# Warm products in the head, two more port users in the planner, and new rank shifts in a planned attention kernel

## The chip, the cores and the metric

The kernel runs on one core of a Trainium2 chip. The metric is the device time of one execution in microseconds (us); of several runs the median is given. A core has five engines that run beside each other: TensorE (PE, matrix products), VectorE (DVE), ScalarE (ACT), GpSimd (POOL) and SyncE (SP, which here only issues transfers).

## The reference

Both branches read the same x (2048 tokens of 512 numbers), and a gate per token mixes them. There are 32 heads of width 16.

```python
g = sigmoid((x * gate_w).sum(-1, keepdims=True))
# branch A: softmax attention
q, k, v = split_heads(x @ A_wqkv)
a = merge(softmax(q @ k.T * 16 ** -0.5) @ v) @ A_wo
# branch B: linear attention with a learned feature map
q, k, v = split_heads(x @ B_wqkv)
phi = lambda t: concat(softmax(t @ w_phi), softmax(-(t @ w_phi)))
kv, z = phi(k).T @ v, phi(k).sum(tokens)
b = merge(phi(q) @ kv / (phi(q) @ z + 1e-6)) @ B_wo
out = g * a + (1 - g) * b
```

The bulk is in branch A: 32 heads x 2048 x 2048 scores, each to be exponentiated.

## The kernel before, in words

**Units.** The scores are cut into units: 128 keys by 512 queries of one head. Four units (four heads, one in each strip of 32 rows of TensorE) for one tile of keys are a "pack"; 16 packs make a group, and there are 32 groups (4 blocks of queries by 8 sets of four heads). A unit takes a score product (`_scores`, L1015), an exponential, and a value product (`_values`, L1122).

**Two ways to the exponential.** Most units go through ScalarE, two at a time: `_qk` makes a score group of two units in the banks 0 to 3 of the accumulation memory, `_exp` (L1063) exponentiates both in one instruction. Score group k waits for exponential k-2, whose bank it takes over. The other units, 488 of 2048, go through VectorE: one instruction (L922) turns a score tile into the bits of a 16-bit float, and steps on four tiles at a time (L947) refine them; the value products then read the tiles `vs`. `NUMS` says how many units of each group take this way. The first score groups are made by halves of the 512 queries, since x lands in halves.

**The head.** `_warm` (L689) issues nine products that nobody reads while the first half of x is on its way. `_proj_k0` (L706) and `_proj_q0` (L745) project keys and queries of the first 512 tokens in two halves of four products each. ScalarE and VectorE (L757, L753) bring the queries into `qT`, VectorE casts the keys into `kT` (L735; later tiles of keys by L770).

**Padding.** Where the planner believes that TensorE has done too little in the last 3 us, it puts up to two products that nobody reads into a score group (`o.pad`, L1035), from score group `PADK` on; they are issued after the group's wait. Within the value products it adds quartets with zero weights (`_fill`, L1129).

**The gate.** `_gate` projects x onto `gate_w`: `gw` is spread to `gwb` by a VectorE copy (L832), four products and transposes follow, an exponential, and at last four small VectorE copies (L862, named `gate_b`) into `ghB`, which branch B reads in its second half.

**The planner.** The order of all instructions is not written by hand. Every step becomes an operation with an engine, an estimated duration, a rank (`prio`, mostly the number of the pack by which it is due) and what it depends on. `order` (a list scheduler) plays all five engines with these estimates, and takes the operation that could start first; among those ready at the same time, the one of the lowest rank. VectorE and GpSimd share a port to the on-chip memory: an operation of GpSimd, or one of VectorE whose name is in `PORT`, starts in the plan only when the last such one has ended. `shift` adds a pseudo-random amount of up to 1, 2 or 3 to the ranks, drawn by one seed in `SEEDS` for each 16 packs of rank (0: no shift). What comes out is a fixed queue for each engine; the waits between them are semaphores, worked out from the dependences. So any change of a rank, a duration or a rule redeals the order from that point on.

Of the kernel before, what the change touches and what calls it, by code (L numbers as in the profile page):

```python
# [10 lines left out]
P = 128  # L11
# [54 lines left out]
class Plan:  # L66
# [43 lines left out]
    def op(self, eng, fn, cost, reads=(), writes=(), deps=(), name="", prio=0.0, rel=-99, kind="full",  # L110
           acquire=None, release=None, lat=None, array=None, strips=None, also=None):
        o = Op(eng, fn, cost, name, prio, rel, kind, self.LAT[eng] if lat is None else lat)
        found = {}
        for b in reads:
            for w in b.writers:
                found[id(w)] = w
        for b in writes:
            for w in b.readers or b.writers:
                found[id(w)] = w
            if b.readers:  # L120
                for w in b.writers:
                    found[id(w)] = w
        for d in deps:
            if d is not None:
                found[id(d)] = d
        found.pop(id(o), None)
        o.deps = list(found.values())
        for b in reads:
            b.readers.append(o)
        for b in writes:  # L130
            b.writers, b.readers = [o], []
        o.acquire, o.release, o.also = acquire, release, also
        o.strips = strips
        o.port = eng == "POOL" or eng == "DVE" and name in self.PORT
        o.held = eng == "PE" and acquire is None and name in self.HOLDING
        o.array = cost if array is None else array
        self.ops.append(o)
        return o

    SEEDS = (6713, 8236, 795, 8928, 4203, 3987, 4548, 4431, 3369, 6855, 1992, 9096, 3816, 673, 8476, 4153, 2488, 5053, 9892, 380, 9864, 6961, 8928, 7398, 8610, 6258, 6732, 8778, 7190, 2318, 6568, 0, 527, 0)  # L140

    def shift(self):
        count = {}
        for o in self.ops:
            k = count[o.name] = count.get(o.name, 0) + 1
            s = self.SEEDS[min(max(int(o.prio // 16), 0), 33)] if o.prio >= 0 else 0
            if s:
# [26 lines left out]
    SAME = 100  # L174
    OPEN = 2
    HURRY, FREE = 20, 30
    PORT = ("v_step", "b_neg", "b_max", "b_sub", "b_sum", "b_total", "b_mul", "n_mul", "n_den", "kvbd")
    HOLDING = ("kproj", "qproj", "bv", "pq", "vproj", "outa", "outb", "wtr", "xtr")

    def rank(self, o):  # L180
# [227 lines left out]
class _Kernel:  # L408
# [18 lines left out]
    VMIN = 8  # L427
    FAST = 3
    VSOON = -2
    PADK = 8  # L430
    LAST, FIRST_OUT, NEXT_OUT, DEP_OUT = 0, 8, 0, 2
    ALONE, EARLY = 12, 10
    PVP = 10
# [248 lines left out]
        job.bank = bank  # L682
        return job, (job if bank is None else None)

    def _warm(self, n, after):

        def run(e):
            for _ in range(n):
                ins = e.matmul(self.ps[:, 4, :], self.warm[:, 0:P], self.warm[:], start=True, stop=True)  # L689
            return ins  # L690
        self.plan.op("PE", run, 0.427 * n, reads=[self.b_warm], deps=[after], name="warm", prio=-99)

    COLS = 0

# [44 lines left out]
    def _proj_q0(self, half, bank):  # L739

        lo, op, ends = 256 * half, self.plan.op, []
        job, pool = self._job(bank)
        m = None
        for c in range(4):
            m = op("PE", lambda e, c=c: e.matmul(self._bank(job)[:, 0:256], self.WA[:, 0, c, 0:P],  # L745
                                                 self.xT[:, c, lo:lo + 256], start=(c == 0), stop=(c == 3)),
                   self.c_pe(256), reads=[self.b_x0[half], self.b_WA[0][0]], deps=[m], name="qproj", prio=half - 2.2,
                   acquire=None if c else pool)
            m.urgent = half - 99
        for side in range(2):  # L750
            dst, by = self.qT[:, side, lo:lo + 256], self.mask[:, side:side + 1]
            if half or side:
                o = op("DVE", lambda e, dst=dst, by=by: e.tensor_scalar(dst, self._bank(job)[:, 0:256], by, None,  # L753
                                                                        op0=ALU.mult), self.c_dve(256) + 0.06,
                       deps=[m] + ends, reads=[self.b_mask], name="q0_ev", prio=side - 2, release=pool if side else None)
            else:
                o = op("ACT", lambda e, dst=dst, by=by: e.activation(dst, self._bank(job)[:, 0:256], ACT.Copy, scale=by),  # L757
                       self.c_act(256) + 0.1, deps=[m], reads=[self.b_mask], name="q0_ev", prio=-2)
            self.b_qT[side].writers.append(o)
            if side == 0:  # L760
                self.b_q0[half].writers.append(o)
            ends.append(o)
        self.early.setdefault(bank, []).extend(ends)

    def _proj_k(self, cp, j):
        due = 32 * cp + 3 * j - self.KDUE if cp else 4 * j - 2.0
        self._proj(lambda c: self.WA[:, 1, c, P * cp:P * cp + P],
                   lambda c: self.xT[:, c, QCH * j:QCH * j + QCH],
                   [self.b_xT[j], self.b_WA[1][cp > 0]],
                   [lambda e, b: e.tensor_copy(self.kT[:, cp, QCH * j:QCH * j + QCH], b)],  # L770
                   self.c_dve(512), due, due - (24 if cp else 99), "kproj", [self.b_kT[cp][j]],
                   urgent=32 * cp + 4 * j - self.SOON)
# [92 lines left out]
                prio=100))  # L865
        self.b_gB.writers = done

    NUMS = (6, 10, 12, 14, 14, 15, 13, 16, 13, 20, 17, 13, 16, 13, 19, 21, 10, 18, 12, 16, 19, 13, 17, 16, 15, 20, 12, 19, 17, 16, 23, 13)

    def _plan_vector(self):  # L870

        NT, away = self.NT, []
        for g in range(self.NPACK // NT):
            n = self.NUMS[g]
            rest = self.REND if g == self.NPACK // NT - 1 else self.REST
# [151 lines left out]
    def _qk(self, a, b, half=None):  # L1027
# [22 lines left out]
        o.on_commit = commit  # L1050
        o.pad = k >= self.PADK
        self.qks.append(o)
# [594 lines left out]
```

## Time and profile before

| | |
|---|---|
| median of 3 runs | 767.77 us (766.18 to 769.58) |
| the profiled execution's own time | 767.62 us |
| its span, first to last instruction | 765.6 us |
| mean granted TensorE clock | 0.997 |
| busy: PE, ACT, DVE, POOL | 97%, 98%, 93%, 27% of the span |
| exponentials of scores on ACT | 782 |
| score tiles by DVE (L922) | 488 |

A row of a group of instructions gives line, engine, operation, output and input, count, then busy time and mean length of one, then the idle time of the engine ahead of them and what ended it. A row of the timeline gives start, length, engine, line and count of instructions merged. A row of a window gives its bounds and length, then for each engine the busy time and count, then the granted clock, the share of the transfer engines and the bandwidth. A wait's row gives who waited for whom: total, times, longest. In rows of one line or tile, three numbers with slashes are the shortest, median and longest duration in ns. A product's end is modelled, so products overlap in the rows.

### The profile page before, as it was taken

The page shows a single profiled execution, that of the slowest core. Times are in us where ns is not written, and L with a number is a line of the kernel's source. Part 1 is how long each engine was busy: PE and PEld are TensorE (multiplying, and loading weights), DVE is VectorE, ACT ScalarE, POOL GpSimd, SP SyncE. Part 2 cuts the span into 40 slices and gives each one's busy share as a digit, 9 for nine tenths or more (in the row PEclk, how much of TensorE's full clock was granted, in tenths as well). Part 3 has the DMA queues.
Part 4 walks back from the last instruction along what each step waited for, and adds up shares of the span by engine and source line. Part 5 has one row for each costly group of instructions (what it writes and reads, how often), then busy time and mean ns, then how long its engine had stood idle before and what let it go on. Part 6 is the DMA issues. An engine that isn't in the chain of part 4 may idle for free.

```text
span 765.6 us, 17042 instructions
## 1 busy us (share of the span) xinstructions
PE 739.6 (97%) x7149; PEld 219.6 (29%) x7220; DVE 711.6 (93%) x1110; ACT 749.1 (98%) x804; POOL 207.5 (27%) x301
## 2 busy tenths in 40 slices
PE   8999999999999999999999999999999999999998
PEld 3322233222222222222332322232222222222222
DVE  4778997899999999999999999999999999999995
ACT  6999999999999999999999999999999999999996
POOL 2210255315053260405145023422314140250000
PEclk9999999999999999999999999999999999999999
DMA  9501001000000000010121202211111121011000
GB/s 232 127 2 28 3 14 15 1 2 8 9 3 14 1 3 14 1 15 2 15 29 28 53 11 51 45 27 30 32 26 28 29 47 24 15 30 27 5 12 28
DMA packets 89180, 20.78 MB, mean 27 GB/s; under 512 B 83472, under 2 KB 88592, under 8 KB 89104
## 3 DMA queue, kind: packets, MB, share of 16 engines
q1 hardware_dynamic: 87232, 18.92, 13.4%
q8 instruction: 56, 0.92, 0.5%
q10 hardware_dynamic: 1872, 0.79, 0.4%
q14 instruction: 20, 0.16, 0.1%
HBM read 4.21 MB, written 2.10 MB: 8 GB/s over the span
## 4 chain that ended last, share of the span: by engine, by line
ACT 76%; PE 15%; DVE 9%; issue 1%
ACT ET L1063 73%; PE ps L1015 5%; PE ps L1122 5%; PE ps L698 3%; ACT bq L1310 3%; DVE vs L922 3%; DVE vs L947 2%; PE ps L1129 1%; PE ps L689 1%; DVE onB L1475 1%; DVE T L1143 0%; DVE bq L1307 0%; DVE btree L1304 0%; DVE ghB L862 0%; DVE qtmp L783 0%
## 5 line engine op out<-in xcount | busy, mean ns | idle before, releaser
L1063 ACT ACTIVATE ET<-ps 128x1024 bf16<-128x1024 f32 (+1 forms) x782 | 720.4, 1154 | 3.7 <-PE ps L1015 3.6
L922 DVE TENSOR_SCALAR vs<-ps 128x512 uint16<-128x512 f32 x488 | 313.7, 679 | 20.7 <-PE ps L1015 19.7
L1015 PE MATMUL ps<-qT,kT 32*128 32x512 bf16 (+1 forms) x2052 | 312.4, 385 | 13.1 <-ACT ET L1063 8.0
L947 DVE TENSOR_SCALAR vs<-vs 128x2048 uint16<-128x2048 uint16 (+1 forms) x244 | 235.4, 977 | 1.9 <-PE ps L1122 0.5
L1122 PE MATMUL ps<-vs,V 128*32 128x512 bf16 x1952 | 216.4, 384 | 1.4 <-DVE vs L947 1.4
L1122 PE MATMUL ps<-ET,V 128*32 128x512 bf16 x1560 | 194.5, 387 | 0.1
L1015 PEld LDWEIGHTS ps<-qT,kT 32*128 32x128 bf16 x2052 | 78.0, 91 | 309.3 <-ACT ET L1063 293.2
L1314 POOL TENSOR_TENSOR btree<-btree 128x512 f16<-128x512 f16 (+1 forms) x32 | 33.4, 1044 | 188.8 <-DVE btree L1312 188.0
L1122 PEld LDWEIGHTS ps<-ET,V 128*32 128x32 bf16 x1560 | 48.9, 94 | 84.1 <-issue 75.8
L1129 PE MATMUL ps<-kT,zero 128*32 128x512 bf16 x628 | 63.4, 385 | 0.0
L1122 PEld LDWEIGHTS ps<-vs,V 128*32 128x32 bf16 x1952 | 49.8, 95 | 45.9 <-issue 27.5
L1299 POOL TENSOR_SCALAR bq<-bq 128x1024 bf16<-128x1024 bf16 x16 | 21.5, 1341 | 150.6 <-DVE bq L1281 119.5
L698 PE MATMUL ps<-WB,xT 128*128 128x512 bf16 x160 | 49.6, 383 | 2.8 <-issue 2.1
L1160 POOL TENSOR_TENSOR T<-T,rinv 128x512 bf16<-128x512 f32 x15 | 18.2, 1210 | 83.4 <-DVE rinv L1158 83.2
L698 PE MATMUL ps<-xT,WA 128*128 128x512 bf16 x101 | 33.2, 392 | 1.9 <-issue 1.6
L788 POOL TENSOR_SCALAR qT<-qtmp,mask 128x512 bf16<-128x512 bf16 x30 | 25.8, 866 | 28.8 <-DVE qtmp L783 28.5
L1143 DVE STREAM_TRANSPOSE T<-ps 128x512 f32<-128x512 f32 x32 | 22.6, 707 | 11.2 <-PE ps L1122 11.1
L1310 ACT ACTIVATE bq<-bq 128x2048 bf16<-128x2048 bf16 x16 | 32.1, 2007 | 0.2
L1281 DVE CAST bq<-ps 128x512 bf16<-128x512 f32 x32 | 21.7, 680 | 0.3 <-PE ps L698 0.2
L826 POOL TENSOR_SCALAR V<-V 128x544 bf16<-128x544 bf16 x16 | 12.6, 788 | 33.4 <-DVE V L819 33.2
L698 PEld LDWEIGHTS ps<-WB,xT 128*128 128x128 bf16 x192 | 13.3, 97 | 25.3 <-issue 20.5
L1129 PEld LDWEIGHTS ps<-kT,zero 128*32 128x32 bf16 x628 | 14.7, 94 | 19.7 <-issue 18.8
(88 smaller groups left out, 405.3 us busy)
## 6 DMA issues: line engine op xcount, KB each, us to landing
T<-T SPq DMA_DIRECT2D x240, 8.0 KB, 1.8
WB<-in_B_wqkv_dram SPq DMA_DIRECT2D x1, 1536.0 KB, 7.9
out_dram<-WB SPq DMA_DIRECT2D x12, 128.0 KB, 1.7
WA<-in_A_wqkv_dram SPq DMA_DIRECT2D x2, 384.0 KB, 5.4
WoB<-in_B_wo_dram SPq DMA_DIRECT2D x1, 512.0 KB, 3.8
WoA<-in_A_wo_dram SPq DMA_DIRECT2D x1, 512.0 KB, 4.8
WA<-in_A_wqkv_dram ACTq DMA_DIRECT2D x2, 128.0 KB, 3.1
WA<-in_A_wqkv_dram ACTq DMA_DIRECT2D x1, 256.0 KB, 4.6
```

What stands on the lines that cost most here:

```text
L698: return e.matmul(out, lhs, rhs, start=start, stop=stop)
L788: x = self.plan.op("POOL", lambda e, side=side: e.tensor_scalar(self.qT[:, s0 + side, :], tmp, self.mask[:, side:side + 1], 0.0, op0=ALU.m ...
L922: bits = lambda e, to, src: e.tensor_scalar(to, src, SCALE * LOG2E * 128.0, float(ORIGIN), op0=ALU.mult, op1=ALU.add)
L947: o = op("DVE", lambda e, k=k, src=src, dst=dst: e.tensor_scalar(dst, src, float(STEPS[k - 1]), None, op0=ALU.add), 0.16 + k * n * QCH * 0 ...
L1015: return e.matmul(out[:, cols], self.kT[32 * i:32 * i + 32, cp, kt * TOK:(kt + 1) * TOK], self.qT[32 * i:32 * i + 32, s, cols], start=True ...
L1063: o = plan.op("ACT", lambda e: e.activation(self.ET[:, a % NS:a % NS + n, cols], self.ps[:, a % NR:a % NR + n, cols], ACT.Exp, scale=SCALE ...
L1122: ins = e.matmul(self._bank(ot)[32 * i:32 * i + 32, :], v[:, v0:v0 + 32], tile, start=(kt == 0), stop=(kt == self.NT - 1), tile_position=( ...
L1129: ins = e.matmul(self._bank(ot)[32 * i:32 * i + 32, :], self.zero[:], self.kT[:, 0, 0:QCH], start=False, stop=False, tile_position=(0, 32 ...
L1143: t1 = op("DVE", lambda e: e.transpose(T1[:, side].rearrange("p b s -> p (b s)"), src()), 0.735, deps=last, writes=[b_T1[side]], name="n_t ...
L1281: [lambda e, b, k=k: e.tensor_copy(bq[:, k].rearrange("p (g s v) -> p g s v", g=8, s=2)[:, :, 0, :], b.rearrange("p (g v) -> p g v", g=8))],
L1310: op("ACT", lambda e: e.activation(flat, flat, ACT.Exp), 1.789, reads=[b], writes=[b], name="b_exp", prio=due + 1)
L1314: + [("b_sum", two(128 * n), lambda e, n=n: e.tensor_tensor(half[:, :, 0:n], half[:, :, 0:n], half[:, :, n:2 * n], ALU.add), (n <= self.P_ ...
```

## The change

It does five things:

- `_proj_q0` adds, after the four products of the first half, an operation of three warm products into bank 1 (`WARM = 3`, rank -2.15, estimated at 0.215 us each). The first score group that uses bank 1 depends on it; both are on TensorE, so no semaphore is waited for.
- `gate_b` and `gwb` join the names in `PORT`.
- `PADK` goes from 8 to 2, so padding is allowed from score group 2 on.
- All 34 seeds of the rank shifts are other ones.
- `NUMS` moves one unit from group 16 to group 15 and one from group 31 to group 30 (counted from 0); the total stays 488.

```diff
-    SEEDS = (6713, 8236, 795, 8928, 4203, 3987, 4548, 4431, 3369, 6855, 1992, 9096, 3816, 673, 8476, 4153, 2488, 5053, 9892, 380, 9864, 6961, 8928, 7398, 8610, 6258, 6732, 8778, 7190, 2318, 6568, 0, 527, 0)
+    SEEDS = (4012, 8099, 2555, 4405, 246, 6853, 8703, 3994, 8542, 8480, 8579, 1442, 8131, 8756, 6763, 9811, 0, 3602, 7438, 1689, 2615, 6046, 0, 2892, 1945, 7535, 9937, 2713, 4648, 6479, 9995, 0, 4360, 0)
...
-    PORT = ("v_step", "b_neg", "b_max", "b_sub", "b_sum", "b_total", "b_mul", "n_mul", "n_den", "kvbd")
+    PORT = ("v_step", "b_neg", "b_max", "b_sub", "b_sum", "b_total", "b_mul", "n_mul", "n_den", "kvbd", "gate_b", "gwb")
...
-    PADK = 8
+    PADK = 2
...
-    def _warm(self, n, after):
+    def _warm(self, n, after, bank=4, cost=0.427, prio=-99):
 
         def run(e):
             for _ in range(n):
-                ins = e.matmul(self.ps[:, 4, :], self.warm[:, 0:P], self.warm[:], start=True, stop=True)
+                ins = e.matmul(self.ps[:, bank, :], self.warm[:, 0:P], self.warm[:], start=True, stop=True)
             return ins
-        self.plan.op("PE", run, 0.427 * n, reads=[self.b_warm], deps=[after], name="warm", prio=-99)
+        return self.plan.op("PE", run, cost * n, reads=[self.b_warm], deps=[after], name="warm", prio=prio)
+
+    WARM = 3
...
         self.early.setdefault(bank, []).extend(ends)
+        if self.WARM and not half:
+            self.early.setdefault(1, []).append(self._warm(self.WARM, m, bank=1, cost=0.215, prio=-2.15))
...
-    NUMS = (6, 10, 12, 14, 14, 15, 13, 16, 13, 20, 17, 13, 16, 13, 19, 21, 10, 18, 12, 16, 19, 13, 17, 16, 15, 20, 12, 19, 17, 16, 23, 13)
+    NUMS = (6, 10, 12, 14, 14, 15, 13, 16, 13, 20, 17, 13, 16, 13, 19, 22, 9, 18, 12, 16, 19, 13, 17, 16, 15, 20, 12, 19, 17, 16, 24, 12)
```

In the order that is built, the queue of TensorE grows by 19 products: the three warm ones and four quartets of `_fill`. The pads in score groups stay three in number, two of them now in score group 4 and one late, where before there was one in each of three late groups. The numbers of instructions on the other engines stay, and their order differs almost everywhere.

## The prediction, made before the changed kernel ran

> **What bounds the kernel now.** I read the page first: the shares of the engines, the chain that ended last, the costliest groups.
>
> ```profile
> span 765.6 us, 17042 instructions
> ...
> PE 739.6 (97%) x7149; PEld 219.6 (29%) x7220; DVE 711.6 (93%) x1110; ACT 749.1 (98%) x804; POOL 207.5 (27%) x301
> ...
> ACT 76%; PE 15%; DVE 9%; issue 1%
> ...
> L1063 ACT ACTIVATE ET<-ps 128x1024 bf16<-128x1024 f32 (+1 forms) x782 | 720.4, 1154 | 3.7 <-PE ps L1015 3.6
> ```
>
> ScalarE (ACT) is busy for 98% of the span and owns 76% of the chain; one kind of instruction, the exponential of a pair of score tiles, is 720 of its 749 us. Next I asked what ACT waited for, over the whole run.
>
> ```profile
> ACT xT L1596 <- remote: 3.8, 1, 3.8
> ACT ET L1063 <- PE ps L1015: 3.6, 6, 1.4
> ACT qT L757 <- PE ps L745: 3.5, 1, 3.5
> ACT L657 <- issue: 2.3, 1, 2.3
> ```
>
> So 9.6 us lie at the two ends (table load, first projection, last output) and only 3.6 us in six waits between. But "busy" hides something: exponentials overlap, and one that starts a little late still counts as busy without a break. The timeline gives the true pace, and the grouped lines of 18 to 757 us the load:
>
> ```profile
> 720.02 14.78 ACT L1063 ACTIVATE ET<-ps 128x1024 bf16<-128x1024 f32 x16
> 734.49 2.15 ACT L1063 ACTIVATE ET<-ps 128x1024 bf16<-128x1024 f32 x2
> ...
> L1063 ACT ACTIVATE ET<-ps 128x1024 bf16<-128x1024 f32 x772 | 712.4, 1158 | 2.1 <-PE ps L1015 2.1
> L1310 ACT ACTIVATE bq<-bq 128x2048 bf16<-128x2048 bf16 x16 | 32.1, 2007 | 0.2
> ```
>
> Sixteen exponentials stand between the starts 720.02 and 734.49: 0.904 us each, undisturbed. 772 of them make 697.9 us. The 16 long ones take 2.007 us less the overlap of about 0.25 that the others show (1.158 - 0.904), an estimate of 1.75, together 28.0. That is 726 of the 739 us in this stretch (739.0 = 757 - 18): some 13 us are lost to late starts, of which 2.1 show as waits. This, the head and the tail are all that a change of order can touch. The built order of the changed kernel holds the same 782 exponentials, 16 long ones and 488 VectorE (DVE) tiles, so ACT's own work stays. TensorE (PE) gets 3 warm products and 4 more filler quartets; both are off the path except where I price them.
>
> **Part one, the head: warm products, and padding from the second score group on.**
>
> ```profile
> 1.45 4.02 PE L689 MATMUL ps<-warm 128*128 128x512 bf16 x9 [1.45 <-DVE warm L620]
> 5.30 1.04 PE L706 MATMUL ps<-xT,WA 128*128 128x256 bf16 x4
> 6.13 1.57 PE L745 MATMUL ps<-xT,WA 128*128 128x256 bf16 x8
> ...
> 7.89 0.28 PE L1015 MATMUL ps<-qT,kT 32*128 32x256 bf16 x2
> ...
> 8.22 3.17 ACT L1063 ACTIVATE ET<-ps 128x512 bf16<-128x512 f32 x5 [0.47 <-PE ps L1015]
> 11.94 2.10 ACT L1063 ACTIVATE ET<-ps 128x1024 bf16<-128x1024 f32 x2 [0.55 <-PE ps L1015]
> 14.54 3.84 ACT L1063 ACTIVATE ET<-ps 128x1024 bf16<-128x1024 f32 x4 [0.50 <-PE ps L1015]
> ...
> 7.02:10.43 3.41, 2.76 (x21) 1.30 (x21) 2.00 (x4) 2.69 (x6) 0.00 (x0) 1.00 1.11 235
> 10.43:13.85 3.42, 3.42 (x13) 0.89 (x12) 1.46 (x4) 2.81 (x3) 0.00 (x0) 0.50 1.08 223
> 13.85:17.26 3.41, 3.26 (x26) 1.47 (x26) 2.05 (x4) 2.91 (x4) 0.65 (x1) 1.00 1.10 294
> ...
> 758.32 1.04 PE L698 MATMUL ps<-WoB,WT 128*128 128x512 bf16 x4
> ```
>
> The granted clock is 1.00 in 7.02 to 10.43, falls to 0.50 in the next 3.4 us and is 1.00 from then on. A 512-column product is issued every (1.04 - 0.39)/3 = 0.22 us at full clock (0.39 is the length of a lone one, as in the rows at 91.04 below), and took about 0.45 (4.02/9) at the start. In the half-clock stretch ACT loses time: from 11.94 to 14.54 it starts two exponentials, 2.60 us instead of 1.81, and before 11.94 it idles 0.55. With the overlap hidden there (about 0.12) that is some 1.45 us.
>
> The new products stand in PE's queue between the query projection of the first half of x and that of the second. At full clock they take 0.65 us, of which about 0.1 falls into the pause before the second half of x is in. The first score product (7.89) needs only the first half, and ahead of it three 256-column products now stand instead of six, so I put its delay at 0.1; the second half, and the third exponential with it, comes about 0.25 later. Two pads are built into the fifth score group, behind its wait for an exponential, not ahead of it: 2 x 0.22 = 0.43 on the path there, and the last three products of the second half of the keys (three of four) are moved behind them. In return the stretch from 7.02 to 10.43 gets 0.65 + 0.43 us of dense array work, and I expect the clock not to drop. Gain 1.45, less 0.25 and 0.43 with some 0.3 of knock-on: **-0.5 us**. Bounds: -1.2 (the delays fall into waits that exist anyway) and +1.0 (the clock drops all the same, the products run at the half rate, 3 x 0.45, and the pads at 0.45 each).
>
> The Trainium skill, page "TensorE: Matmul & The Clock Gate", Part 1 on the HAM clock gate, has the array fall back to half rate only after a whole idle window of about 3.4 us. This trace disagrees: the drop at 10.43 follows a stretch in which PE shows 2.76 of 3.41 us busy. By that rule the warm products would change no clock; the rival below works that out. The same section says that the window runs freely of the kernel's start; no run here shows that, and if so the head's gain differs between executions.
>
> **Part two, the gate's copies and the shared port.** The largest wait of ACT in the body, 1.4 us, has a visible cause:
>
> ```profile
> L1349 POOL TENSOR_SCALAR eps<-bsum,ghB x16: 290/291/1122, 388.8 to 677.9; 128x32 f32<-128x32 f32 x16
> ...
> L862 DVE COPY ghB<-gh x4: 165/406/936, 89.9 to 91.8; 32x16 f32<-32x16 f32 x4
> ...
> 89.97 1.06 POOL L1160 TENSOR_TENSOR T<-T,rinv 128x512 bf16<-128x512 f32 x1 [0.62 <-DVE rinv L1158]
> 91.00 0.69 POOL L788 TENSOR_SCALAR qT<-qtmp,mask 128x512 bf16<-128x512 bf16 x1
> ...
> 89.92 2.01 DVE L862 COPY ghB<-gh 32x16 f32<-32x16 f32 x4
> 91.95 0.69 DVE L770 CAST kT<-ps 128x512 bf16<-128x512 f32 x1
> ...
> 91.04 0.39 PE L1015 MATMUL ps<-qT,kT 32*128 32x512 bf16 x2
> 92.70 0.38 PE L1015 MATMUL ps<-qT,kT 32*128 32x512 bf16 x1 [1.28 <-DVE kT L770]
> ...
> 94.20 1.02 ACT L1063 ACTIVATE ET<-ps 128x1024 bf16<-128x1024 f32 x1 [1.39 <-PE ps L1015]
> ```
>
> Four tiny copies take 2.01 us instead of 4 x 0.165 = 0.66: the long ones lie beside two GpSimd (POOL) instructions. Behind them in DVE's queue is the cast of a key tile; PE has a score product queued that needs it and waits 1.28 us; all score products behind wait too, and ACT idles 1.39. With gate_b among the port's users the planner starts these copies only when it believes POOL idle. In the built order they stand as two, one and one between other DVE work, the key casts that were behind them now ahead, and their first reader (L1349) starts at 388.8. **-1.4 us**; bounds -1.6 (with 0.25 of hidden overlap) and 0 (POOL runs late and they collide as before). The gwb copy is once, 0.5 us, and held nobody: zero.
>
> **Part three, new shifts, and one tile moved forward twice** (NUMS: group 15 to 22 from 21, group 30 to 24 from 23, the next group one less). The pads first:
>
> ```profile
> L1035 PEld LDWEIGHTS ps<-kT x3: 95/95/95, 392.2 to 717.4; 128*128 128x128 bf16 x3
> ...
>   ACT ET L1063: 1.6, 3
> ```
>
> Three padded score groups stand in the body, each behind its wait for ACT, so each pad is 0.22 us on the path. The built order keeps one: **-0.4 us** (bounds 0, -0.6).
>
> The rest of the body's loss, 13 - 1.6 - 0.6, about 10.8 us, is redealt. Most of it is small (772 starts, some 14 ns each) and stays with the same planner and the same work. The lumps are drawn anew; the largest beside the copies:
>
> ```profile
> 471.16 0.40 PE L1122 MATMUL ps<-vs,V 128*32 128x512 bf16 x4 [0.63 <-DVE vs L947]
> ...
> 471.93 1.94 ACT L1063 ACTIVATE ET<-ps 128x1024 bf16<-128x1024 f32 x2 [0.55 <-PE ps L1015]
> ...
> 708.00:726.00 18.00, 16.96 (x192) 4.41 (x185) 17.79 (x28) 18.00 (x21) 1.05 (x1) 1.00 0.04 5
> 726.00:744.00 18.00, 17.92 (x199) 4.62 (x196) 17.72 (x27) 18.00 (x21) 0.00 (x0) 1.00 0.09 13
> 744.00:757.00 13.00, 12.65 (x114) 3.57 (x117) 9.47 (x16) 13.00 (x15) 0.00 (x0) 1.00 0.00 1
> ```
>
> A value product waits for DVE, the score products behind it wait, ACT loses 0.55. DVE is full where a tile is added: 0.49 us idle in 708 to 744. A tile costs it about 1.1 (711.6 us of DVE hold 488 tiles and other work; one tile is about 0.65 of eviction and 0.5 of its share of the steps, an estimate). But 3.5 us lie idle in 744 to 757, and tiles may be done ahead. I take **0** for the redeal, from -2 (a fifth of the 10.8 gone) to +2.8 (two lumps like the copies').
>
> **Sum.** -0.5 - 1.4 - 0.4 + 0 = -2.3 us. The profiled execution took 767.62 (span 765.6 and 2.0 around it), the median is 767.77, 0.15 above: the forecast is 767.77 - 2.3, **765.5 us**.
>
> **Rivals.** A measurement of this kernel tells about 0.5%, 3.8 us, from no change: below 763.9 is faster, above 771.6 slower.
> - *Smoother order (0.20), 763.2.* As forecast, and the redeal removes a fifth of the remaining loss. For it: 10.8 us are there, and the port is now planned better. Against it: no edit aims at those small losses.
> - *The clock was not the warm products' to keep (0.15), 766.9.* The drop comes anyway, or would not have come by the page's rule: the head costs +0.9, the rest stays: 767.77 + 0.9 - 1.4 - 0.4. For it: PE was already 81% busy in the stretch before the drop.
> - *New lumps (0.12), 768.5.* The port's waits go, but one lump of 1.4 and three of 0.55 (3.0) come, most at DVE's full groups.
> - *Slower (0.08), 772.1.* DVE at 93% is late for its steps, and the wait seen at 471, once, appears in a dozen of the 32 groups of heads: 12 x 0.55 = 6.6, less 2.3. It decides from eleven on (6.1 us). For it: DVE's 98 to 99% before 744. Against: of 3.6 us of ACT waits only this one shows it.
> - That the change does nothing is out: every engine's queue is another.
>
> **Numbers.** The forecast has 0.45. Faster 0.20, slower 0.08, the other three, 0.72, within 0.5%. The range 763.0 to 769.2 holds the forecast, the second and third rival and half of the first (the best of all bounds, 767.77 - 1.2 - 1.6 - 0.6 with some of the redeal, is below it); about 0.18 is left out.
>
> **What would show it.** Right: a clock row of 1.00 from 7.02 on, the eighth exponential by 14.1 instead of 14.54; gate copies near 0.17 each, no wait of 1.4 in the body; one pad row in the body. Wrong: 0.50 in the second stretch; a copy of 0.9 us followed by a wait of PE; waits of PE for the DVE steps (L947) summing to well over 1.4 us; ACT's waits for score products above 3.6 us; or a start of the first exponential after 8.6.

## The result and the profile after

| | before | after |
|---|---|---|
| median | 767.77 us (766.18 to 769.58, 5 runs) | 764.04 us (763.30 to 764.15, 5 runs) |
| ratio of the times | | 0.9947, 95% interval 0.9927 to 0.9967 |
| profiled execution, its span | 767.62, 765.6 us | 764.15, 762.2 us |
| mean granted clock in the profiled execution | 0.997 | 1.000 |

The change took 3.7 us off, just under the 0.5% that the prediction called no change, and inside its range. Most of the prediction's terms can now be measured one by one, and two of them, the head and the new order, were misjudged. The page of the changed kernel, the same parts as before (line numbers above about 690 move by two to four):

```profile
span 762.2 us, 17153 instructions
...
PE 750.7 (98%) x7239; PEld 220.1 (29%) x7239; DVE 709.5 (93%) x1110; ACT 748.0 (98%) x804; POOL 205.0 (27%) x301
...
ACT 76%; PE 21%; DVE 2%; issue 0%
...
L1067 ACT ACTIVATE ET<-ps 128x1024 bf16<-128x1024 f32 (+1 forms) x782 | 720.1, 1164 | 1.6 <-PE ps L1019 1.5
```

The work of ACT is the same, 782 exponentials. Its idle time fell from 16.5 to 14.2 us, and its busy time, in which late starts hide, from 749.1 to 748.0. The waits of ACT say where it idles now:

```profile
ACT xT L1600 <- PE ps L700: 3.6, 1, 3.6
ACT qT L759 <- PE ps L747: 3.6, 1, 3.6
ACT L657 <- issue: 2.3, 1, 2.3
ACT ET L1067 <- PE ps L1019: 1.5, 3, 0.7
```

Six waits for score products, 3.6 us, have become three, 1.5 us. All three are in the head. From 18 to 754 us the grouped line of the exponentials shows what is left in the body, 0.1 us where it was 2.1:

```profile
L1067 ACT ACTIVATE ET<-ps 128x1024 bf16<-128x1024 f32 x772 | 712.4, 1168 | 0.1
```

The head, by the timeline of ACT and by windows laid along the clock's steps of this execution:

```profile
8.55 2.17 ACT L1067 ACTIVATE ET<-ps 128x512 bf16<-128x512 f32 x4 [0.65 <-PE ps L1019]
11.25 1.02 ACT L1067 ACTIVATE ET<-ps 128x1024 bf16<-128x1024 f32 x1 [0.54 <-PE ps L1019]
12.59 5.60 ACT L1067 ACTIVATE ET<-ps 128x1024 bf16<-128x1024 f32 x6 [0.32 <-PE ps L1019]
...
7.17:10.59 3.42, 2.96 (x20) 1.16 (x18) 1.93 (x4) 2.52 (x5) 0.00 (x0) 1.00 1.12 219
10.59:14.00 3.41, 3.32 (x22) 1.29 (x20) 1.78 (x4) 2.56 (x4) 0.00 (x0) 1.00 1.00 207
```

The clock stays at 1.00, as forecast. But the two pads cost more than their 0.43 us: the fifth exponential starts at 11.25, 2.70 after the first, and the sixth waits until 12.59 for the keys whose products stand behind the pads. No wait of PE or ACT shows behind the gate's copies any more, though they still take 1.2 us together instead of 0.66 (the longest took 0.575, so the mark of 0.17 each was not met); what they still cost, the last experiment measures:

```profile
L866 DVE COPY ghB<-gh 32x16 f32<-32x16 f32 x4 | 1.2, 296 | 0.1
```

### The profile page after: what moved, and what is told of

The parts are those of the page before. It is cut to its first block, busy times and chain, and to the rows that moved or that the text cites. A ratio compares the mean times of both kernels' runs of the same rounds, so it can differ in the third digit from the quotient of the medians.

```text
span 762.2 us, 17153 instructions
## 1 busy us (share of the span) xinstructions
PE 750.7 (98%) x7239; PEld 220.1 (29%) x7239; DVE 709.5 (93%) x1110; ACT 748.0 (98%) x804; POOL 205.0 (27%) x301
## 4 chain that ended last, share of the span: by engine, by line
ACT 76%; PE 21%; DVE 2%; issue 0%
ACT ET L1067 72%; PE ps L1019 7%; PE ps L1126 7%; PE ps L700 4%; ACT bq L1314 4%; PE ps L813 1%; DVE vs L926 1%; PE ps L1133 1%; DVE vs L951 1%; PE ps L689 1%; PE ps L1245 0%; PE ps L708 0%; DVE onB L1479 0%; PE ps L747 0%; PE ps L1039 0%
## 5 line engine op out<-in xcount | busy, mean ns | idle before, releaser
L1126 PE MATMUL ps<-ET,V 128*32 128x512 bf16 x1560 | 196.7, 387 | 0.3 <-DVE vs L926 0.2
L1133 PE MATMUL ps<-kT,zero 128*32 128x512 bf16 x644 | 65.1, 385 | 0.0
L700 PE MATMUL ps<-WB,xT 128*128 128x512 bf16 x192 | 59.9, 384 | 0.0
L700 PE MATMUL ps<-xT,WA 128*128 128x512 bf16 x120 | 38.1, 384 | 0.0
L792 POOL TENSOR_SCALAR qT<-qtmp,mask 128x512 bf16<-128x512 bf16 x30 | 24.2, 813 | 33.5 <-DVE qtmp L787 31.7
```

What stands on the lines that cost most here:

```text
L700: return e.matmul(out, lhs, rhs, start=start, stop=stop)
L792: x = self.plan.op("POOL", lambda e, side=side: e.tensor_scalar(self.qT[:, s0 + side, :], tmp, self.mask[:, side:side + 1], 0.0, op0=ALU.m ...
L1126: ins = e.matmul(self._bank(ot)[32 * i:32 * i + 32, :], v[:, v0:v0 + 32], tile, start=(kt == 0), stop=(kt == self.NT - 1), tile_position=( ...
L1133: ins = e.matmul(self._bank(ot)[32 * i:32 * i + 32, :], self.zero[:], self.kT[:, 0, 0:QCH], start=False, stop=False, tile_position=(0, 32 ...
```

## The experiments

Two kinds of kernel follow. In the first the planner runs as it did, and single instructions are then moved, added or emptied in the finished queues: all else keeps its place. In the second a setting is changed and the planner deals the whole order anew. The time of every kernel is compared with runs of the kernel before on the same chip.

**How before itself varies.** These comparisons gave 56 runs of before, and their time falls into steps by the mean granted clock of the run:

| mean clock of the run | runs of before | median | range |
|---|---|---|---|
| 0.999 to 1.000 | 8 | 766.55 us | 766.16 to 766.97 |
| 0.997 to 0.998 | 26 | 767.70 us | 767.30 to 768.25 |
| 0.995 to 0.996 | 19 | 769.26 us | 768.87 to 769.60 |
| 0.993 | 3 | 770.75 us | 770.62 to 770.89 |

One stretch of 3.4 us at half clock is 3.4 x 0.5 / 766 = 0.0022 of the mean. So 48 of 56 runs held one or more such stretches, each worth 1.1 to 1.6 us, and the program without one takes 766.55. Below, "undisturbed" means the runs of a kernel at 0.999 or more. The kernels ran on three chips; the runs of before with one stretch have medians of 767.6, 767.7 and 767.8 on them, so differences of some 0.2 us between kernels are not to be read. Only the profiled execution of a kernel shows where its stretches lie.

**The gate's copies alone, moved by one step** (queues of before, four instructions moved):

```diff
+            q = p.queues["DVE"]
+            late = [o for o in q if o.name == "gate_b"]
+            q = [o for o in q if o.name != "gate_b"]
+            at = [k for k, o in enumerate(q) if o.name == "n_t1"][2]
+            p.queues["DVE"] = q[:at] + late + q[at:]
```

> The order of before, kept as it is on every engine; only the four gate copies on VectorE are taken from ahead of the key cast and put ahead of the third transpose of the normalization (about 114 us), where GpSimd and VectorE both idled. Theory (the copies, held at the port, delayed the cast, PE and ACT): the four copies near 0.17 us each, the pair of exponentials at 91.6 and 94.2 comes back to 0.90 us apart, no wait of ACT over 0.8 us in the body, time 1.4 to 1.7 us below before. Rival (the cast was late for another reason, or the gain is given back later): the gap shrinks below 1 us or opens elsewhere, time within 0.5 us of before.

Measured: 766.17 us (ratio 0.9981, 0.9966 to 0.9997), undisturbed 765.87. Only 0.7 of the 1.6 came. The place was badly chosen: the transpose I meant, near 114 us, is the next one, and the copies landed before the transpose at 91.0. The queues show the wait moved on to it; rows of DVE, then of PE:

```profile
88.66 0.69 DVE L775 CAST kT<-ps 128x512 bf16<-128x512 f32 x1
89.27 0.54 DVE L1309 TENSOR_TENSOR btree<-btree 128x256 bf16<-128x256 bf16 x1
89.84 1.15 DVE L867 COPY ghB<-gh 32x16 f32<-32x16 f32 x4
91.02 0.72 DVE L1148 STREAM_TRANSPOSE T<-ps 128x512 f32<-128x512 f32 x1
...
90.75 0.39 PE L1020 MATMUL ps<-qT,kT 32*128 32x512 bf16 x2
91.80 0.39 PE L1020 MATMUL ps<-qT,kT 32*128 32x512 bf16 x1 [0.66 <-DVE T L1148]
```

The cast is early now, and the copies sit ahead of a transpose that frees a bank; a score product for VectorE waits for that bank, and everything on PE behind it.

**The same, to the fourth transpose** (`[3]` for `[2]` in the diff above):

> The order of before once more, the four gate copies now put ahead of the fourth transpose of the normalization (near 114 us, where VectorE waits 1.6 us and GpSimd idles), so that neither a key cast nor the release of a bank stands right behind them. Theory: the gap of ACT at 91 to 93 us shrinks from 1.7 (before) and 1.3 (copies one step later) to under 0.3 us, no run has a half-clock window near 92, time 1.7 to 3 us below before. Rival (PE's queue at 92 us is late for other reasons too): 0.7 us or more of the gap stays, time about as with the copies one step later (766.2).

Measured: 765.16 us (0.9971, 0.9956 to 0.9985); undisturbed 764.90, so 1.65 us below before's 766.55 (1.4 below the median of the four undisturbed runs of before on the same chip). ACT's rows show an unbroken run where the gap of 1.39 was:

```profile
86.09 10.37 ACT L1068 ACTIVATE ET<-ps 128x1024 bf16<-128x1024 f32 x11
```

So the copies are the cause of that lump, and it is worth about what its rows said with the hidden overlap, 1.6 us. Five of twelve runs still had half-clock stretches (766.2 to 767.9), so the ones of the head, or others, remain.

**Warm products and pads in before's order:**

```diff
+            q = p.queues["PE"]
+            at = [k for k, o in enumerate(q) if o.name == "qproj"][3] + 1
+            q.insert(at, Op("PE", lambda e: [e.matmul(self.ps[:, 1, :], self.warm[:, 0:P], self.warm[:], start=True, stop=True)
+                                             for _ in range(3)][-1], 0.645, "warm", 0.0, -99, "full", 0.2))
+            self.qks[4].filled = 2
```

> The order of before, with the three warm products put behind the first half of the query projection and two pads into the fifth score group, nothing else. Theory (the clock falls for want of array work in the head): granted clock 1.00 from about 7 us on, the ninth exponential of pairs 0.2 to 0.6 us earlier than in before, median 0.3 to 0.7 us below before, and a narrower spread of the runs than before's 3.4 us. Rival (idle windows alone bring the clock down, the products only cost): clock 0.50 again for one window, median 0.3 to 1.0 us above before, spread as before.

Measured: 768.18 us (1.0004, 0.9992 to 1.0016), no difference, because two things cancel: 8 of 12 runs were undisturbed, against 8 of 56, but those took 767.86, 1.3 us above before's undisturbed. The other four lay at 769.2 to 771.7, and the profiled one of them shows where; windows along the clock's steps, then PE's wait, then ACT:

```profile
86.08:89.49 3.41, 3.41 (x27) 0.89 (x25) 2.78 (x8) 3.41 (x6) 1.93 (x3) 1.00 0.00 0
89.49:92.91 3.42, 2.14 (x16) 0.55 (x15) 3.30 (x7) 2.62 (x3) 1.51 (x2) 1.00 0.05 5
92.91:96.32 3.41, 3.41 (x25) 0.59 (x23) 2.70 (x5) 2.00 (x2) 0.00 (x0) 0.50 0.15 18
...
92.00 0.38 PE L1020 MATMUL ps<-qT,kT 32*128 32x512 bf16 x1 [1.28 <-DVE kT L775]
...
93.83 1.02 ACT L1068 ACTIVATE ET<-ps 128x1024 bf16<-128x1024 f32 x1 [1.72 <-PE ps L1020]
95.34 1.02 ACT L1068 ACTIVATE ET<-ps 128x1024 bf16<-128x1024 f32 x1 [0.49 <-PE ps L1020]
96.68 1.94 ACT L1068 ACTIVATE ET<-ps 128x1024 bf16<-128x1024 f32 x2 [0.31 <-PE ps L1020]
```

The gate's stall can be followed by half clock too: after a stretch with PE at 2.14 of 3.42 us the next is at 0.50, and ACT idles another 0.8 us. The same wait of 1.28 us stands in the profiled run of before, but there the clock's steps lie elsewhere, and the clock stays at 1.00 in the stretch of the stall and in the next:

```profile
88.94:92.35 3.41, 2.46 (x16) 0.51 (x15) 3.25 (x7) 3.41 (x5) 2.14 (x3) 1.00 0.00 0
92.35:95.77 3.42, 3.07 (x27) 0.91 (x27) 3.39 (x7) 2.03 (x3) 0.00 (x0) 1.00 0.14 14
```

So the copies cost about 1.6 us, and in a run where the steps fall so, some 1 us more (an estimate from those 0.8 us and the overlap that does not show). How busy PE is does not decide alone: 2.46 of 3.41 us kept the clock here, and 2.76 of 3.41 in the head of the same execution did not. What else decides stays open.

**The changed kernel without its new head** (its queues, with the products and pads emptied):

```diff
+            [o for o in p.queues["PE"] if o.name == "warm"][1].fn = lambda e: None
+            self.qks[4].filled = 0
```

> The order of after, without the three warm products and without the two pads of the fifth score group, all else in place. Theory: the clock falls to 0.50 for one window at about 10.5 us; time 0.2 to 1.0 us above after, and its runs spread like before's. Rival (the head is worth nothing, all of the gain is in the body): time within 0.2 us of after or below it, spread as narrow as after's.

Measured: 763.22 us (0.9945, 0.9926 to 0.9965): the rival's median, the theory's spread. Five runs were undisturbed with a median of 763.08, about 1 us better than after; the sixth, at a clock of 0.993, took 767.48. So the head of the change costs 0.8 us in the median, and with the new order the clock mostly held without it.

**Only the pads taken out** (the second line of that diff alone):

> The order of after without the two pads in the fifth score group, the warm products kept. Theory (the warm products alone hold the clock through the head, the pads only cost 0.43 us): mean clock 0.999 to 1.0 in every run, time 0.3 to 0.6 us below after, so 763.4 to 763.8. Rival (the pads are needed): a run in five or so with a clock of 0.997 or less and 1.5 to 4 us more.

Measured: 763.28 us (0.9935, 0.9920 to 0.9950), all six runs undisturbed. The pads cost 0.76 us and buy nothing that shows. The warm products cost 0.2 (763.28 against 763.08), which is within the scatter. Whether they keep the clock is not settled: in this order 0 of 11 runs with them had a half-clock stretch and 1 of 6 without. Over all kernels with the new seeds it is 0 of 22 against 4 of 13, but three of those four are from another deal (the seeds alone, below).

**The port users alone** (planner deals anew):

```diff
-    PORT = ("v_step", "b_neg", "b_max", "b_sub", "b_sum", "b_total", "b_mul", "n_mul", "n_den", "kvbd")
+    PORT = ("v_step", "b_neg", "b_max", "b_sub", "b_sum", "b_total", "b_mul", "n_mul", "n_den", "kvbd", "gate_b", "gwb")
```

> Before, with only the two names added to the planner's port users; the order is replanned with the old seeds. Theory (the rule removes the gate's collision, the rest is dealt anew around zero): the wait of 1.4 us is gone, time 0 to 3 us below before. Rival (the old seeds fitted the old plan and another deal is worse): the collision is gone but other lumps come, time 1 us or more above before.

Measured: 783.87 us (1.0190, 1.0166 to 1.0214). Four of five runs held half-clock stretches (0.988 to 0.994); the fifth, undisturbed, took 779.04, still 12.5 above before's 766.55. The copies do what the rule wants, and ACT's waits show that the rest fell apart; below them, ACT's last exponentials and VectorE's last refining step:

```profile
L862 DVE COPY ghB<-gh 32x16 f32<-32x16 f32 x4 | 0.7, 164 | 0.1
...
ACT xT L1596 <- PE ps L698: 11.4, 1, 11.4
ACT ET L1063 <- PE ps L1015: 7.1, 13, 1.3
...
ACT ET L1063 <- PE ps L1122: 2.0, 1, 2.0
...
750.40 14.10 ACT L1063 ACTIVATE ET<-ps 128x1024 bf16<-128x1024 f32 x15 [1.99 <-PE ps L1122]
...
768.16 1.22 DVE L947 TENSOR_SCALAR vs<-vs 128x4096 uint16<-128x4096 uint16 x1
```

The copies take 0.164 us each. But the wait of the last output went from 3.8 to 11.4 us: VectorE is still at its tiles (to 769.4) when ACT has done its last exponential (764.5). The gate's copies lie some 660 us earlier; what differs here is the deal.

**The new seeds and the two moved tiles alone** (planner deals anew, old port users, no warm products or early pads):

```diff
-    SEEDS = (6713, 8236, 795, 8928, 4203, 3987, ...
+    SEEDS = (4012, 8099, 2555, 4405, 246, 6853, ...
-    NUMS = (... 19, 21, 10, ... 16, 23, 13)
+    NUMS = (... 19, 22, 9, ... 16, 24, 12)
```

> Before with only the new seeds and the two moved tiles; port users, padding and warm products as before, the order replanned. Theory (seeds are fitted to one plan and worth nothing in another): other lumps come, time from 1 us below to 15 us above before. Rival (the new seeds are good as such and carry the gain): 763.5 to 765.5 us, as after.

Measured: 763.90 us (0.9956, 0.9937 to 0.9975), undisturbed 763.44; three of seven runs at 766.1 with a clock of 0.996. My theory fell: here the rival holds. ACT's waits between the ends are all but gone:

```profile
ACT xT L1596 <- PE ps L698: 3.6, 1, 3.6
...
ACT ET L1063 <- PE ps L1015: 0.8, 1, 0.8
ACT bq L1310 <- DVE bq L1307: 0.3, 1, 0.3
```

The seeds, with the two moved tiles, carry the body's gain without the port rule. They give even the whole change in the median: 763.90 with them alone, 764.04 with all five edits. What the two moved tiles do by themselves was not tried. The copies collide here as well (one takes 0.55 us), but only a wait of 0.3 us follows, that of ACT for the VectorE step behind them.

**Two unpicked deals**, the changed kernel with other seeds (planner deals anew):

```diff
+    SEEDS = (0,) * 34
...
+    SEEDS = tuple(range(1000, 1034))
```

> After with all seeds zero, so the ranks are not shifted; replanned, all else as after. An unselected deal. Theory (the seeds of before and of after are both picked among many deals, an unpicked one is worse): 3 to 20 us above after. Rival (deals differ little, as the prediction took it, -2 to +2.8 us): within 3 us of after.

> After with 34 arbitrary seeds (1000 to 1033), replanned, all else as after: a second unselected deal. Theory (unpicked deals are worse): 3 to 20 us above after, with a lump at the last groups of VectorE tiles or in the tail. Rival: within 3 us of after.

Measured: 791.47 us (1.0312, 1.0293 to 1.0331) and 802.58 us (1.0447, 1.0433 to 1.0462): 27 and 39 us above after. ACT's waits with zero seeds:

```profile
ACT ET L1067 <- PE ps L1126: 13.8, 3, 6.4
ACT xT L1600 <- PE ps L700: 11.4, 1, 11.4
ACT ET L1067 <- PE ps L1019: 3.4, 5, 1.3
```

Three waits behind value products are 13.8 us, one of them 6.4 at 756 us, where VectorE is full; the tail is 7.8 above after's 3.6. The window ahead of that wait:

```profile
744.00:757.00 13.00, 10.58 (x95) 3.03 (x97) 13.00 (x20) 6.65 (x8) 1.91 (x1) 0.97 0.02 3
```

The mean clocks of the runs, 0.986 to 0.995, say that a few us of both distances are half-clock stretches. So the two sets of seeds that the kernels came with lie at the good end of a wide range, as far as three other deals (these two, and the port users alone) can show it. How they were found no run shows.

**Gate copies late and warm products together, in before's order** (the diffs of the fourth transpose and of the three products, without the pads):

> The order of before with the gate copies ahead of the fourth transpose and, besides, the three warm products behind the first half of the query projection; no pads, no new seeds. Theory (half-clock windows come from too little array work in the head and from the stall at 92 us, and both are now gone): mean clock 0.999 to 1.0 in all runs or all but one, spread under 1.5 us, median 765.0 to 765.5, against runs of the same order without the products, half of which lay 1.3 to 3 us above 764.9. Rival (the windows fall by chance, whatever the products): a third or more of the runs at a clock of 0.998 or less.

Measured: 765.16 us (0.9965, 0.9953 to 0.9977); undisturbed 764.88 in 9 of 12 runs, three at 767.5 to 768.0 with a clock of 0.996. Nine of 12 against 7 of 12 without the products is no difference that so few runs can show, and it is not the theory's all but one: it stays open where those stretches lie, since the profiled run had none.

**A head with the keys early.** The timeline of after shows the sixth exponential waiting for a cast whose products stand behind the pads. Without pads, with those three products ahead of the third score group and their cast ahead of the first tile:

```diff
+            self.qks[4].filled = 0
+            q = p.queues["PE"]
+            k = [o for o in q if o.name == "kproj"][4:8]
+            rest = [o for o in q if o not in k[1:]]
+            at = rest.index(k[0]) + 1
+            p.queues["PE"] = rest[:at] + k[1:] + rest[at:]
+            q = p.queues["DVE"]
+            ev = [o for o in q if o.name == "kproj_ev"][1]
+            q.remove(ev)
+            q.insert([o.name for o in q].index("v_bits"), ev)
```

> The order of after without the two pads, and with the other three products of the second half of the keys moved ahead of the third score group (where PE waits for VectorE) and their cast ahead of the first tile of VectorE. Theory (the sixth exponential waits for that cast): it starts 0.6 to 0.9 us earlier against the first exponential than in after (4.04 us there), time 0.8 to 1.2 us below after, 762.8 to 763.3, clock 1.0. Rival (VectorE or the next keys become the bound of the head): less than 0.4 us below the kernel without pads.

Measured: 762.84 us (0.9929, 0.9914 to 0.9944), 1.2 below after, 0.44 below the kernel without pads; all six runs undisturbed. The head of ACT is one unbroken row:

```profile
8.33 10.62 ACT L1077 ACTIVATE ET<-ps 128x512 bf16<-128x512 f32 x13 [0.66 <-PE ps L1029]
```

**That kernel with the gate's copies moved to a quiet place:**

```diff
+            late = [o for o in q if o.name == "gate_b"]
+            q = [o for o in q if o.name != "gate_b"]
+            at = [k for k, o in enumerate(q) if o.name == "kproj_ev"][12] + 1
+            p.queues["DVE"] = q[:at] + late + q[at:]
```

> The kernel with the keys early and without the two pads, and the four gate copies moved behind the key cast near 121 us, where GpSimd idles. Theory (three of the copies still lie beside GpSimd near 99 us in after and cost ACT some 0.4 us): copies 0.17 us each, time 0.2 to 0.4 us below the kernel with the keys early, 762.4 to 762.7. Rival (those lags are not the copies'): no difference, 762.8.

Measured: 762.45 us (762.43 to 762.68; 0.9926, 0.9914 to 0.9938), the copies at 167 ns. The 0.39 us agree with the theory, though the two kernels ran on different chips and single runs of the other come down to 762.41. If so, the copies cost time in after too, without any wait that shows. It is the fastest kernel of the study, 1.6 us below after.

## Why the prediction was right, and where it was not

Chained through the undisturbed runs, the 3.73 us are these. The steps of 0.2 us are as small as the scatter of a kernel's own runs. The first row is not the new head's doing alone: the new order without it has that row too.

| step | from, to | worth | forecast |
|---|---|---|---|
| half-clock stretches that the median no longer holds | 767.77, 766.55 | -1.22 | as a gain of 1.45 in the head's term |
| the gate's copies out of the way | 766.55, 764.90 | -1.65 | -1.4 (-1.6 to 0) |
| the rest of the new deal | 764.90, 763.08 | -1.82 | 0 (-2 to +2.8), and -0.4 for late pads |
| three warm products | 763.08, 763.28 | +0.20 | +0.25 |
| two early pads | 763.28, 764.04 | +0.76 | +0.43, and 0.3 of knock-on |

*The head (-0.5).* This step failed, in its gain. The costs were near: 0.2 for the products and 0.76 for the pads, where 0.98 was forecast for all. But I read one stretch at half clock from one profile and took it as a fixed part of the program, which the products would remove. It is a chance: before has such a stretch in 48 of 56 runs, once or several times; one trace has it in the head, one at the gate's stall. In before's order the products and pads made it rarer (4 of 12 runs against 18 of 21 on the same chip), but cost 1.3 us in the undisturbed runs, and the median stayed (768.18, before 768.25 on that chip). In the new order 5 of 6 runs were undisturbed without them, so there was little left to gain, and the head came out as a loss of 0.8 us. Of the expected marks the clock held, 1.00 from 7.17 on, as it did in the profiled run without products and pads; the eighth exponential started at 14.41, not by 14.1. The forecast's upper bound of +1.0 is about the three costs at full rate (0.25, 0.43 and 0.3); at the half rate that stands beside it, it would have been more.

*The gate (-1.4).* Right in the cause and near in size (1.65, or 1.4 on one chip); but not for the reason that the change gives. The rule on the port removes the collision at the price of a deal that cost 12 to 16 us with the old seeds, and the new seeds remove the stall without the rule. In after the copies still collide. That the copies stand elsewhere is the cause; the rule was neither needed nor enough.

*The redeal (0, from -2 to +2.8).* This step failed too. The value, -1.82, came out at the edge of its bounds, and the bounds were wrong: the deal of the new rule with the old seeds came out 16 us above before (12.5 undisturbed), two unpicked deals 27 and 39 us above after. I had reasoned that the same planner with the same work would lose about the same, and priced the range by the lumps of one trace. But that trace belonged to a picked deal; its lumps are not what another deal has. The late pads (-0.4) were not tried by themselves and are in this row. The rival "smoother order" (763.2; its own sum gives 763.3) came nearest in time: 1.8 of the 10.8 us went, where it took a fifth, 2.2. Its reason, that the port is planned better, did not hold, since the seeds give as much without the rule. That the total fell inside the range is therefore partly luck: a head that cost instead of gaining was covered by a deal that came out well and in which the clock mostly holds without that head.

*The rival on the clock* (766.9) had the head nearly right: it gave it a loss of 0.9, and the runs show 0.8. Its total missed by the deal.

*The slower rival* had the wrong form. In the bad deals the cost is not a dozen small waits for VectorE's steps but a few long ones at its full groups and in the tail (13.8 and 7.8 us with zero seeds). The rows of DVE in 708 to 744 us, with 0.49 us of idle time, had shown how little room it has.

*The page's rule.* The Trainium skill, page "TensorE: Matmul & The Clock Gate", Part 1, table of the two states, has half rate come back after an idle window of about 3.4 us; the runs disagree a second time, with PE at 2.14 of 3.42 us busy ahead of the drop at 92.91. That its window runs freely of the kernel's start agrees with what the runs now show: the same program has the drop at 10.43 us in one execution, and none in others. The steps of the clock at 10.43 in before and at 92.91 in the run with products and pads also do not lie on one grid: the 82.48 us between them are 24.2 stretches of 3.413.

## What to carry to other kernels

Where a planner with seeds orders the work, treat the order as one picked sample: a change of a rule must be judged with its own seeds, and a single trace does not price another deal. When runs of one program scatter in steps, set each run's time against its mean clock before comparing medians; here a third of the gain was a program that no longer fell to half clock. Try each edit of a set without the others: here the seeds and two moved tiles alone gave what the whole set gave. And when an instruction is moved out of the way, look at what stands behind its new place: one step later the copies blocked a bank instead of a cast.

## What the hardware showed that I had not expected

- A wait of PE of 1.28 us in mid-kernel was followed by half clock for 3.4 us in one execution (0.50 in 92.91 to 96.32, after PE at 2.14 of 3.42 us) and by none in another (1.00 after 2.46 of 3.41). One such stretch costs this kernel 1.1 to 1.6 us.
- Filler work at the start costs its own time (0.2 and 0.76 us here), and what it does for the clock depends on the order: half-clock stretches in 4 of 12 runs against 18 of 21 with products and pads in before's order, 3 of 12 against 5 of 12 with the products alone, 0 of 11 against 1 of 6 in the new one.
- Copies of 0.17 us grew to 0.94 beside a GpSimd instruction. Where PE waited for what was queued behind them, that cost about 1.6 us; where no wait showed, 0.39.
